# Reordering the opening of a fused attention and feed-forward kernel: token loads on two queues, fewer zero matmuls, shift products interleaved, scores of the first head moved forward, and the row of the condition vector moved to a later turn

## Chip, cores and metric

One core of a Trainium2 chip. The metric is the device time of one execution in microseconds (us); lower is better.

## The reference, cut to what matters

```python
mod = (_silu(c) @ w_mod).reshape(...)            # c: 1x1024, w_mod: 1024x6144
sa, ca, ga, sb, cb, gb = ...                     # shift, scale, gate of block A; the same of block B
h = _layernorm(x) * (1 + ca) + sa                # x: 2048 tokens x 1024
x = x + ga * attention(h)                        # 32 query heads, 4 key/value heads, last 512 keys
h = _layernorm(x) * (1 + cb) + sb
x = x + gb * swiglu_ffn(h)                       # 3584 wide
```

The opening has to compute the scale `ca` and shift `sa` from `c`, normalise the first 512 tokens, and start the query products of the first heads.

## The kernel before

`T.op(stream, emit, reads, writes)` records one instruction in its engine's stream, and the waits that its buffers demand. In these traces an instruction whose input is late holds up what stands behind it on its engine: in the kernel before TensorE's first instruction waits for the load of `c` until 3.69 us, and the nine zero matmuls behind it begin at 3.87 us. `mm` is one matmul (all at line 268 of the kernel before), `transpose` one TensorE transpose (line 272), `warm(n, b)` is n matmuls of zeros, recorded to keep TensorE busy. A wide matmul has 512 columns (128x512 in the views), a transpose 128, a product with a vector one. PSUM is the memory that matmuls write to, divided into banks (XB, QB and so on); an evacuation is the copy out of a bank, for which the next user of the bank waits here (1.47 us each in two places of the kernel before).

Two things below are called the row of `c`: the load of `c` itself (`c_row`, part 1 of the change), and the row that `row_task` makes of silu(c) for all partitions, with a copy on VectorE (part 5).

The loads, all from one queue:

```python
T.op(Q_x[0], lambda: SP.dma_start(x_res[:, 0, :], xf[0:P, :]), writes=[B_x[0]])
T.op(Q_c, lambda: SP.dma_start(c_row[:, :], c.rearrange("o (k p) -> (o k) p", p=P)), writes=[B_cT])
for t in range(1, TPC):
    T.op(Q_x[t], lambda: SP.dma_start(x_res[:, t, :], xf[t * P:(t + 1) * P, :]), writes=[B_x[t]])
# ... then scale weights (8 x 256 KB), query weights (2 x 512 KB), shift weights (4 x 512 KB), K, V ...
# TensorE's first instruction transposes c:
T.op(PE, lambda: TE.transpose(bank_bf(XB)[:, 0:DT], c_row[:, :], ident[0:DT, 0:DT]), ...)
```

The opening proper (statistics and normalisation on VectorE, GpSimd and ScalarE; transposes, scale products `mod_ca` and zero matmuls on TensorE; cut):

```python
warm(9, WB); stats(0, ...); aggr(0); stats(1, 1, 0); norm(0, 0, 0)
x_first(0)                     # 8 transposes of token tile 0
warm(6, WB) ... x_first(1); warm(2, WB)
for k in range(3):
    mod_ca(k); warm(2, WB)     # mod_ca(k): 8 one-column matmuls
... x_first(2) ... mod_ca(3), mod_ca(4) ... x_first(3) ... mod_ca(5..7)
warm(5, WB)
x_mod()                        # read the scale, evacuate the transposes into hT
```

Query products of heads 0 to 3 without the shift, then the shift products, then the shift is added to `hT` and its effect on the four queries (a bias `bq`, 32 one-column matmuls) to the queries:

```python
QB0 = [PVB, PVB + 1, SCB, QB]
for kc in range(DT):
    for h in range(LEAD + 1):
        mm(bank(QB0[h]), wq_s[0][:, kc, h * P:(h + 1) * P], hT[0][:, kc, :], ...)
for k in range(DT):
    mod_mm(wsa[:, k, :], B_wsa[k], k, MCOLS)           # shift products, 64 one-column matmuls
T.op(DVE, ... mod_bf[:, 0:DT] <- bank XB)              # "shift read", line 627
k_turn(0, SCB + 1)                                     # transposes of K
... 32 bias products; shift additions on VectorE (4), ScalarE (2), GpSimd (2); evacuations of the 4 queries
```

The turns of the attention loop. "Turn i" below is the value of `i`:

```python
rows = row_task(sc_row, B_scr, sc_bf[:, :], B_sc)      # silu(c) as a row on all partitions
bg.append(rows)
for i in range(1, NA + 2):
    ...
    if 2 <= i < 1 + Hkv:
        k_turn(i - 1, XB)                              # K transposes, PSUM bank XB
    if i == 5:
        add_ln1(1)                                     # normalisation of the next 512 tokens, in background
    if i + LEAD < NA:
        if (i + LEAD) % Hq == 0:
            finish(ln1[(i + LEAD) // Hq])
        qproj(i + LEAD, SCB + 3 if i == 1 else QB)     # 8 matmuls and an evacuation on VectorE
    ...
    if 0 <= i - 1 < NA:
        scores(i - 1)                                  # 4 matmuls, exponentials on ScalarE
    if 0 <= i - 2 < NA:
        pv(i - 2)                                      # 16 matmuls of 129 columns
    run_bg(1)                                          # one step of the first background task
```

`row_task` also puts its products into bank XB: four 128-column matmuls, then a copy on VectorE (line 584), twice.

The softmax here doesn't subtract the row's maximum and nothing guards it: scores larger than these inputs give would overflow.

Of the kernel before, what the change touches and what calls it, by code (L numbers as in the profile page):

```python
# [3 lines left out]
ALU = mybir.AluOpType  # L4
# [3 lines left out]
P = 128  # L8
# [122 lines left out]
def bass_adaLN_cond__sliding_block_cached__swiglu_ffn__prompt_kernel(  # L131
# [87 lines left out]
    def bank(b, n=512, off=0):  # L219
        return ps[:, b * 512 + off:b * 512 + off + n]  # L220
# [32 lines left out]
    QB = 4  # L253
# [4 lines left out]
    with nc.Block() as block:  # L258

        @block.gpsimd  # L260
        def _(g):
# [39 lines left out]
                    xf[ch * CH:(ch + 1) * CH, :].rearrange("(t p) d -> p t d", p=P)),  # L301
                     writes=B_x[ch * TPC:(ch + 1) * TPC])

            T.op(Q_x[0], lambda: SP.dma_start(x_res[:, 0, :], xf[0:P, :]), writes=[B_x[0]])  # L304
            T.op(Q_c, lambda: SP.dma_start(c_row[:, :], c.rearrange("o (k p) -> (o k) p", p=P)), writes=[B_cT])
            for t in range(1, TPC):
                T.op(Q_x[t], lambda: SP.dma_start(x_res[:, t, :], xf[t * P:(t + 1) * P, :]), writes=[B_x[t]])


            OFF_WO = 0  # L310
# [90 lines left out]
            def stats(t, sl, hf):  # L401
                T.op(DVE, lambda: V.bn_stats(st_[sl][:, hf * 6:hf * 6 + 6], x_res[:, t, hf * 512:hf * 512 + 512]),  # L402
                     reads=[B_x[t]], writes=[B_st[sl]])

            def aggr(sl):
                T.op(DVE, lambda: V.bn_aggr(mv[sl][:, :], st_[sl][:, :]), reads=[B_st[sl]], writes=[B_mv[sl]])  # L406
                T.op(POOL, lambda: g.tensor_scalar(rstd[sl], mv[sl][:, 1:2], eps, None, op0=ALU.add),  # L407
                     reads=[B_mv[sl]], writes=[B_rs[sl]])
                T.op(POOL, lambda: g.tensor_tensor(rstd[sl], rstd[sl], mhalf[:, 0:1], ALU.pow),  # L409
                     reads=[B_rs[sl], B_mh], writes=[B_rs[sl]])  # L410

            def norm(t, sl, ns):
                T.op(DVE, lambda: V.tensor_scalar(nsc4[ns], x_res[:, t, :], mv[sl][:, 0:1], rstd[sl],  # L413
                                                  op0=ALU.subtract, op1=ALU.mult),
                     reads=[B_x[t], B_mv[sl], B_rs[sl]], writes=[B_ns4[ns]])
# [41 lines left out]
            def warm(n, b):  # L457
                for _ in range(n):
                    mm(bank(b), zwarm[:, 0:P], zwarm, True, True, [B_zw], PB[b])
# [22 lines left out]
            def mod_ca(k):  # L482
                mod_mm(wca[k], B_wca[k], k, MCOLS)
# [3 lines left out]
            T.op(ACT, lambda: A.activation(nsc4[tl], x_res[:, tl, :], AF.Copy, accum_out=acc[:, 0:1]),  # L487
                 reads=[B_x[tl]], writes=[B_ns4[tl], B_acc])
            WB = PVB
            warm(9, WB)  # L490
            stats(0, 0, 0)
            stats(0, 0, 1)
            aggr(0)
            stats(1, 1, 0)
            norm(0, 0, 0)
            x_first(0)
            warm(6, WB)
            stats(1, 1, 1)
            aggr(1)
            T.op(POOL, lambda: g.tensor_scalar(nmean[:, :], acc[:, 0:1], -1.0 / D, None, op0=ALU.mult),  # L500
                 reads=[B_acc], writes=[B_nm])
            T.op(ACT, lambda: A.activation(nsc4[tl], x_res[:, tl, :], AF.Square, bias=nmean[:, 0:1], accum_out=acc[:, 1:2]),
                 reads=[B_x[tl], B_nm], writes=[B_ns4[tl], B_acc])
            stats(2, 2, 0)
            norm(1, 1, 1)
            x_first(1)
            warm(2, WB)
            for k in range(3):
                mod_ca(k)
                warm(2, WB)  # L510
            stats(2, 2, 1)
            T.op(DVE, lambda: V.bn_aggr(mv[2][:, :], st_[2][:, :]), reads=[B_st[2]], writes=[B_mv[2]])
            T.op(POOL, lambda: g.tensor_scalar(rstd[2], mv[2][:, 1:2], eps, None, op0=ALU.add),
                 reads=[B_mv[2]], writes=[B_rs[2]])
            T.op(POOL, lambda: g.tensor_scalar(rstd[tl], acc[:, 1:2], 1.0 / D, eps, op0=ALU.mult, op1=ALU.add),
                 reads=[B_acc], writes=[B_rs[tl]])
            T.op(POOL, lambda: g.tensor_tensor(rstd4[:, 2:4], rstd4[:, 2:4], mhalf[:, 0:2], ALU.pow),
                 reads=[B_mh], writes=[B_rs[2], B_rs[tl]])
            norm(2, 2, 2)
            x_first(2)  # L520
            warm(1, WB)
            T.op(DVE, lambda: V.tensor_scalar(nsc4[tl], x_res[:, tl, :], nmean[:, 0:1], rstd[tl],
                                              op0=ALU.add, op1=ALU.mult),
                 reads=[B_x[tl], B_nm, B_rs[tl]], writes=[B_ns4[tl]])
            for k in range(3, 5):
                mod_ca(k)
                warm(1, WB)
            x_first(3)
            for k in range(5, DT):
                warm(1, WB)  # L530
                mod_ca(k)
            warm(5, WB)
            x_mod()


# [59 lines left out]
            qT_s = [arena.at(OFF_QT + i * KB, [CH], BF16, [B_qT[i]]) for i in range(NQT)]  # L595
            Q_tr = [dq("q_tr%d" % i) for i in range(NOS)]

            def qproj(i, b=QB):
                ch, h = divmod(i, Hq)
                gidx = ch * HG + h // 4  # L600
                sl = gidx % NWQ
                hh = h % 4
                for kc in range(DT):
                    mm(bank(b), wq_s[sl][:, kc, hh * P:(hh + 1) * P], hT[ch % 2][:, kc, :], kc == 0, kc == DT - 1,
                       [B_wq[sl][kc // HK], B_hT[ch % 2][kc]], PB[b])
                qs = i % NQT
                T.op(DVE, lambda: V.tensor_copy(qT_s[qs], bank(b)), writes=[PB[b], B_qT[qs]])  # L607



            QB0 = [PVB, PVB + 1, SCB, QB]
            LEAD = 3
            for kc in range(DT):
                for h in range(LEAD + 1):
                    mm(bank(QB0[h]), wq_s[0][:, kc, h * P:(h + 1) * P], hT[0][:, kc, :], kc == 0, kc == DT - 1,
                       [B_wq[0][kc // HK], B_hT[0][kc]], PB[QB0[h]])
            for k in range(DT):
                mod_mm(wsa[:, k, :], B_wsa[k], k, MCOLS)

            def k_turn(gk, b):  # L620
                for kt in range(KT):
# [6 lines left out]
            k_turn(0, SCB + 1)  # L628
            kd, ks = k_evac(0, SCB + 1)
            T.op(ACT, lambda: A.activation(kd, ks, AF.Copy), writes=[PB[SCB + 1], B_kT[0]])  # L630
            for h in range(LEAD + 1):
                for kc in range(DT):
                    mm(bank(SCB + 2, 1, 2 * h), wq_s[0][:, kc, h * P:(h + 1) * P], mod_bf[:, kc:kc + 1],
                       h == 0 and kc == 0, kc == DT - 1, [B_wq[0][kc // HK], B_mode], PB[SCB + 2], skip=True)
            for dt in range(DT):
                d = hT[0][:, dt, :]
                if dt < 4:
                    T.op(DVE, lambda: V.tensor_scalar(d, d, mod_bf[:, dt:dt + 1], None, op0=ALU.add),  # L638
                         reads=[B_mode], writes=[B_hT[0][dt]])
                elif dt < 6:  # L640
                    T.op(ACT, lambda: A.activation(d, d, AF.Identity, bias=mod_bf[:, dt:dt + 1]),
                         reads=[B_mode], writes=[B_hT[0][dt]])
                else:
                    T.op(POOL, lambda: g.tensor_scalar(d, d, mod_bf[:, dt:dt + 1], None, op0=ALU.add),
                         reads=[B_mode], writes=[B_hT[0][dt]])
            T.op(DVE, lambda: V.tensor_copy(bq[:, :], psap((SCB + 2) * 512, [[2, LEAD + 1]])), writes=[PB[SCB + 2], B_bq])  # L646
            for h in (0, 2, 3, 1):
                if h < 2:
                    T.op(DVE, lambda: V.tensor_scalar(qT_s[h], bank(QB0[h]), bq[:, h:h + 1], None, op0=ALU.add),
                         reads=[B_bq], writes=[PB[QB0[h]], B_qT[h]])  # L650
                else:
                    T.op(ACT, lambda: A.activation(qT_s[h], bank(QB0[h]), AF.Identity, bias=bq[:, h:h + 1]),
                         reads=[B_bq], writes=[PB[QB0[h]], B_qT[h]])

            B_ex = [_Buf("ex%d" % i) for i in range(NEX)]
            ex_s = [arena.at(OFF_EX + i * 4 * KB, [KT, CH], BF16, [B_ex[i]]) for i in range(NEX)]
# [90 lines left out]
            LOADX = {19: 2, 40: 3}  # L747
            LOADT = {Hq + 2 + (9 * n) // 4: n for n in range(NL)}
            LOADO = {5 + (21 * p) // 8: p for p in range(8)}
            rows = row_task(sc_row, B_scr, sc_bf[:, :], B_sc)  # L750
            bg.append(rows)
            for i in range(1, NA + 2):
                ch, h = divmod(i, Hq)
                if i % 4 == 1:
# [7 lines left out]
                if 2 <= i < 1 + Hkv:  # L762
                    k_turn(i - 1, XB)
                    kd, ks = k_evac(i - 1, XB)
                    T.op(DVE, lambda: V.tensor_copy(kd, ks), writes=[PB[XB], B_kT[i - 1]])
                    if i == Hkv:
                        for b_ in B_hT[1]:
                            for kb in B_kn:
                                b_.absorb(kb)
                if i == 5:  # L770
                    add_ln1(1)
                if h == 2 and 1 <= ch < NCH - 1:
# [3 lines left out]
                if i + LEAD < NA:  # L776
                    if (i + LEAD) % Hq == 0:
                        finish(ln1[(i + LEAD) // Hq])
                    qproj(i + LEAD, SCB + 3 if i == 1 else QB)
                if 7 <= i < 7 + DT:  # L780
                    mod_mm(wga[:, i - 7, :], B_wga[i - 7], i - 7, GCOLS)
                    if i == 6 + DT:
# [18 lines left out]
                    oproj_mm(NCH - 1, 0, QB, 8 * n, 8 * n + 8)  # L801
                elif n >= 3:
                    oproj_mm(NCH - 1, 1, XB, 8 * (n - 3), 8 * (n - 3) + 8)
                if 0 <= i - 1 < NA:
                    scores(i - 1)
                if 0 <= i - 2 < NA:
                    pv(i - 2)
# [154 lines left out]
```

## Time and profile before

| | kernel before |
|---|---|
| median of 3 runs | 1283.01 us (1282.88 to 1283.18) |
| span of the profiled execution | 1282.1 us (that execution took 1283.94) |
| TensorE busy | 1264.0 us, 99% |
| first TensorE instruction | 3.69 us |
| first query product | 17.53 us |
| shift read | 27.03 us |
| K transposes of turn 4 | 44.13 us |

The page of the kernel before: its span, the busy time of each engine (us, share of the span, instructions), and from its fourth part the shares of the chain that ended last:

```profile
span 1282.1 us, 17720 instructions
...
PE 1264.0 (99%) x7513; PEld 646.4 (50%) x7655; DVE 477.4 (37%) x881; ACT 340.2 (27%) x384; POOL 44.5 (3%) x103
...
PE 98%; issue 1%; DVE 1%; DMA 0%; SPq 0%
```

TensorE is the bound, and it is on the chain nearly always. A change can only win where TensorE waits, does something useless or runs at a lower clock; that is the opening. The chain of waits of the kernel before, in order of time (start us, length us, what held the chain):

```profile
1.18 2.46 DMA c_row<-in_c_dram
...
3.87 3.95 PE ps L268 x9
...
17.53 0.59 PE ps L268 x2
...
37.12 0.69 DVE arena L689
37.81 0.61 DVE arena L584
...
38.55 0.38 PE ps L272 x4
...
48.06 6.94 PE ps L268 x55
```

The chain begins with the wait for the row of `c` (2.46 us); nine zero matmuls take 3.95 us, 0.44 us each, against 0.216 us later, so they ran at half the later speed (called cold below). At 37.1 and 42.5 us the chain leaves TensorE: it waits for two VectorE operations in a row, and the second (line 584) is the copy of the `c` row, after which the K transposes may reuse bank XB. The view of waits of the kernel before for 36 to 46 us (engine, waiting tile and line, what it waited for: us in total, times, longest us) adds this up:

```profile
PE ps L272 <- DVE arena L584: 2.9, 2, 1.5
```

The kernel before in one-microsecond windows (window, length, then for each engine busy us and instruction count, the granted TensorE clock as a share of full speed, DMA share, GB/s):

```profile
28.00:29.00 1.00, 0.86 (x11) 0.34 (x8) 1.00 (x3) 0.98 (x2) 1.00 (x1) 1.00 1.21 260
29.00:30.00 1.00, 0.76 (x3) 0.31 (x4) 0.96 (x4) 0.71 (x2) 1.00 (x2) 0.88 0.59 95
30.00:31.00 1.00, 0.98 (x3) 0.18 (x2) 0.69 (x2) 0.98 (x2) 0.91 (x3) 0.50 0.85 218
31.00:32.00 1.00, 1.00 (x4) 0.30 (x2) 0.68 (x1) 0.85 (x1) 1.00 (x2) 0.50 1.08 384
32.00:33.00 1.00, 1.00 (x6) 0.47 (x4) 0.01 (x1) 0.82 (x1) 1.00 (x3) 0.50 1.09 373
33.00:34.00 1.00, 1.00 (x8) 0.59 (x7) 0.42 (x1) 0.91 (x2) 0.22 (x1) 0.91 1.04 351
```

The clock fell to 0.50 near 29.8 us and was back at 33.2; this is called the half clock below. TensorE was recorded busy for 0.63, 0.74, 0.86 and 0.76 us of the four microseconds from 26 to 30. Half a clock for 3.4 us of 1282 us is 0.13%, so a run with it shows a mean clock of 0.999 and one without it 1.000.

### The profile page before, as it was taken

To read this page: it belongs to the slowest core of one execution; us is meant where nothing else is said; L and a number is where in the kernel's file an instruction comes from. 1 tells how busy PE (TensorE), PEld (TensorE's weight loads), DVE (VectorE), ACT (ScalarE), POOL (GpSimd) and SP (SyncE) were. 2 spreads that over 40 slices of the span, in tenths; PEclk is the share of its full clock that TensorE was granted. 3 is DMA by queue.
4 is the path that set the end of the run, shared out by engine and by line. 5 is a ranking of instruction groups with operands and counts; after the bars stand their busy time and mean duration, and the time that the engine had idled before them with its cause. 6 is when DMAs were issued, how large, how long until landed. Compare 5 with 4: busy or idle time off the path is not lost.

```text
span 1282.1 us, 17720 instructions
## 1 busy us (share of the span) xinstructions
PE 1264.0 (99%) x7513; PEld 646.4 (50%) x7655; DVE 477.4 (37%) x881; ACT 340.2 (27%) x384; POOL 44.5 (3%) x103
## 2 busy tenths in 40 slices
PE   8999999999999999999999999999999999999999
PEld 4565545555445554455554444444444444444444
DVE  4455314765137652265422331233222331221222
ACT  3555402555015551055520111011100111011100
POOL 2120000000000010000000000000000000000000
PEclk9999999999999999999999999999999999999999
DMA  9799402976108841055351974046421654035200
GB/s 316 202 230 272 108 1 40 217 139 148 34 17 162 174 105 46 1 122 118 71 152 60 288 243 131 17 136 176 132 74 34 200 152 131 17 109 170 66 9 25
DMA packets 234830, 155.31 MB, mean 121 GB/s; under 512 B 129024, under 2 KB 220032, under 8 KB 234752
## 3 DMA queue, kind: packets, MB, share of 16 engines
q1 hardware_dynamic: 176512, 95.45, 31.0%
q10 hardware_dynamic: 58240, 58.72, 14.5%
q8 instruction: 60, 0.98, 0.3%
q14 instruction: 18, 0.15, 0.0%
HBM read 119.54 MB, written 4.19 MB: 97 GB/s over the span
## 4 chain that ended last, share of the span: by engine, by line
PE 98%; issue 1%; DVE 1%; DMA 0%; SPq 0%
PE ps L268 98%; PE ps L272 0%; DMA c_row<-in_c_dram 0%; DVE arena L638 0%; DVE arena L689 0%; DVE arena L584 0%; DVE rl L686 0%; DVE tmp L708 0%; DVE arena L710 0%; SPq L304 0%; DVE arena L474 0%; PE ps L393 0%; DVE gain L454 0%; DVE mod_bf L468 0%; DVE gain_f L470 0%
## 5 line engine op out<-in xcount | busy, mean ns | idle before, releaser
L268 PE MATMUL ps<-arena 128*128 128x512 bf16 (+1 forms) x7240 | 1257.3, 333 | 8.0 <-DVE bq L646 0.2
L268 PEld LDWEIGHTS ps<-arena 128*128 128x128 bf16 x7382 | 636.3, 98 | 619.9 <-issue 3.6
L668 ACT ACTIVATE arena<-ps 128x1024 bf16<-128x1024 f32 x256 | 261.9, 1023 | 356.9 <-PE ps L268 345.1
L891 ACT ACTIVATE arena<-ps 128x512 bf16<-128x512 f32 x112 | 66.9, 597 | 506.2 <-PE ps L268 506.2
L892 DVE TENSOR_TENSOR arena<-ps,arena 128x512 bf16<-128x512 f32 x112 | 77.5, 692 | 276.2 <-PE ps L268 276.2
L708 DVE TENSOR_TENSOR tmp<-ps,rowb 128x512 f32<-128x512 f32 (+1 forms) x65 | 44.4, 683 | 319.1 <-PE ps L268 319.1
L607 DVE CAST arena<-ps 128x512 bf16<-128x512 f32 x124 | 85.7, 692 | 58.6 <-PE ps L268 58.6
L689 DVE TENSOR_TENSOR arena<-ps,rl 128x512 bf16<-128x512 f32 x128 | 88.5, 691 | 4.7 <-DVE rl L686 0.2
L686 DVE RECIPROCAL rl<-ps 128x4 f32<-128x4 f32 x128 | 23.3, 182 | 120.4 <-PE ps L268 120.4
L402 DVE BATCH_NORM_STATS2 st<-x_res 128x6 f32<-128x512 bf16 x62 | 42.3, 682 | 3.5 <-DMA x_res<-in_A_x_dram 3.5
L407 POOL TENSOR_SCALAR rstd<-mv 128x1 f32<-128x1 f32 x30 | 6.7, 222 | 911.1 <-DVE mv L406 911.1
L561 DVE SCALAR_TENSOR_TENSOR arena<-arena 128x1024 bf16<-128x1024 bf16 x24 | 29.2, 1215 | 0.0
L710 DVE TENSOR_TENSOR arena<-tmp,x_res 128x512 bf16<-128x512 f32 (+1 forms) x33 | 22.3, 676 | 1.1
L710 DVE TENSOR_TENSOR x_res<-tmp,x_res 128x512 bf16<-128x512 f32 x32 | 22.1, 692 | 1.1
L418 DVE TENSOR_SCALAR arena<-arena,gain,mod_bf 128x512 bf16<-128x512 bf16 x56 | 20.3, 405 | 0.0
L409 POOL TENSOR_TENSOR rstd<-rstd,mhalf 128x1 f32<-128x1 f32 x30 | 17.0, 568 | 2.5
L413 DVE TENSOR_SCALAR nsc<-x_res,mv,rstd 128x1024 bf16<-128x1024 bf16 x30 | 16.1, 538 | 1.0 <-POOL rstd L409 1.0
L576 POOL TENSOR_SCALAR arena<-arena,c 128x128 bf16<-128x128 bf16 x24 | 14.1, 606 | 7.0 <-PE ps L268 6.7
L268 PEld LDWEIGHTS ps<-sc_bf,arena 128*128 128x128 bf16 x192 | 7.1, 96 | 3.4
L268 PE MATMUL ps<-sc_bf,arena 128*128 128x1 bf16 x192 | 7.2, 163 | 0.1
L406 DVE BATCH_NORM_AGGREGATE mv<-st 128x2 f32<-128x12 f32 x30 | 6.3, 209 | 1.0
L272 PE MATMUL ps<-arena 128*128 128x128 bf16 x32 | 2.9, 228 | 2.9 <-DVE arena L584 2.9
(53 smaller groups left out, 42.2 us busy)
## 6 DMA issues: line engine op xcount, KB each, us to landing
arena<-in_A_wq_dram SPq DMA_DIRECT2D x31, 1024.0 KB, 5.7
arena<-in_B_w_gate_dram ACTq DMA_DIRECT2D x28, 1024.0 KB, 5.5
arena<-in_B_w_up_dram ACTq DMA_DIRECT2D x28, 1024.0 KB, 8.1
arena<-in_A_wo_dram SPq DMA_DIRECT2D x8, 1024.0 KB, 6.5
arena<-in_B_w_down_dram SPq DMA_DIRECT2D x7, 1024.0 KB, 8.3
out_dram<-arena SPq DMA_DIRECT2D x15, 256.0 KB, 2.0
x_res<-in_A_x_dram SPq DMA_DIRECT2D x3, 1024.0 KB, 7.5
arena<-in_w_mod_dram SPq DMA_DIRECT2D x8, 256.0 KB, 5.5
```

The lines of the kernel that those rows point to most:

```text
L268: T.op(PE, lambda: TE.matmul(out_ap, lhsT, rhs, start=start, stop=stop, skip_group_check=skip), reads=reads, writes=[bank_buf])
L402: T.op(DVE, lambda: V.bn_stats(st_[sl][:, hf * 6:hf * 6 + 6], x_res[:, t, hf * 512:hf * 512 + 512]), reads=[B_x[t]], writes=[B_st[sl]])
L418: T.op(DVE, lambda: V.tensor_scalar(dst[:, dt, :], dst[:, dt, :], gain[gi][:, dt:dt + 1], mod_bf[:, ccol + dt:ccol + dt + 1], op0=ALU.mult ...
L561: T.op(DVE, lambda: V.scalar_tensor_tensor(mt[n % 2], mt[n % 2], 1.0, sc_row, op0=ALU.mult, op1=ALU.mult, accum_out=mcol[:, n:n + 1]), rea ...
L607: T.op(DVE, lambda: V.tensor_copy(qT_s[qs], bank(b)), writes=[PB[b], B_qT[qs]])
L668: T.op(ACT, lambda: A.activation(ex_s[es][:, 2 * kp:2 * kp + 2, :], banks2(SCB + 2 * kp), AF.Exp, scale=att_scale), writes=[PB[SCB + 2 * k ...
L686: T.op(DVE, lambda: V.reciprocal(rl[r][:, :].rearrange("p (a b) -> p a b", a=2), psap(PVB * 512 + P, [[512, 2], [130, 2]])), writes=both + ...
L689: T.op(DVE, lambda: V.tensor_tensor(o_s[os_].rearrange("p (a b) d -> p a b d", a=2), psap(PVB * 512, [[512, 2], [130, 2], [1, P]]), rlb, A ...
L708: T.op(DVE, lambda: V.tensor_tensor(tmp[s][:, 0:n], bank(b, n), rowb[ri][:, c0:c0 + n], ALU.mult), reads=[B_row[ri]], writes=[PB[b], B_tmp ...
L710: T.op(DVE, lambda: V.tensor_tensor(dst[:, c0:c0 + n], tmp[s][:, 0:n], x_res[:, t, c0:c0 + n], ALU.add), reads=[B_tmp[s], B_x[t]], writes= ...
L891: T.op(ACT, lambda: A.activation(sg_s[ss], bank(gb), AF.Silu), writes=[PB[gb], B_sg[ss]])
L892: T.op(DVE, lambda: V.tensor_tensor(guT[:, ft, :], bank(ub), sg_s[ss], ALU.mult), reads=[B_sg[ss]], writes=[PB[ub], B_gu[ft]])
```

## The change

The intent: get TensorE to the attention loop earlier. Five parts:

1. Token tiles 1 and 3 are loaded from the scalar engine's queue, 0 and 2 from the sync engine's; the row of `c` goes third in the sync queue.
2. 24 zero matmuls instead of 34 in the opening; the statistics of each tile stand together on VectorE.
3. Shift products 0 to 3 go between the query products; five zero matmuls around the bias products; GpSimd has no shift additions any more.
4. In turn 1 the scores of head 0 stand ahead of the fifth query, which uses bank QB instead of a score bank.
5. The row of `c` is made in turn 17 instead of turns 1 to 3.

```diff
-            T.op(Q_x[0], lambda: SP.dma_start(x_res[:, 0, :], xf[0:P, :]), writes=[B_x[0]])
-            T.op(Q_c, lambda: SP.dma_start(c_row[:, :], c.rearrange("o (k p) -> (o k) p", p=P)), writes=[B_cT])
-            for t in range(1, TPC):
-                T.op(Q_x[t], lambda: SP.dma_start(x_res[:, t, :], xf[t * P:(t + 1) * P, :]), writes=[B_x[t]])
+            Q_xa = [dq("q_xa%d" % i, A) for i in range(2)]
+            for t in range(TPC):
+                q = Q_xa[t // 2] if t % 2 else Q_x[t]
+                T.op(q, lambda: (A if t % 2 else SP).dma_start(x_res[:, t, :], xf[t * P:(t + 1) * P, :]), writes=[B_x[t]])
+                if t == 2:
+                    T.op(Q_c, lambda: SP.dma_start(c_row[:, :], c.rearrange("o (k p) -> (o k) p", p=P)), writes=[B_cT])
...  (opening: 34 zero matmuls become 24, not counting the five below; statistics of a tile together; cut)
+            def mod_sa(k2):
+                for k in (2 * k2, 2 * k2 + 1):
+                    mod_mm(wsa[:, k, :], B_wsa[k], k, MCOLS)
+
             for kc in range(DT):
                 for h in range(LEAD + 1):
                     mm(bank(QB0[h]), wq_s[0][:, kc, h * P:(h + 1) * P], hT[0][:, kc, :], kc == 0, kc == DT - 1,
                        [B_wq[0][kc // HK], B_hT[0][kc]], PB[QB0[h]])
-            for k in range(DT):
-                mod_mm(wsa[:, k, :], B_wsa[k], k, MCOLS)
+                if kc == 3:
+                    mod_sa(0)
+                elif kc == 6:
+                    mod_sa(1)
+            mod_sa(2)
+            mod_sa(3)
...
+            warm(2, SCB + 3)
             for h in range(LEAD + 1):
                 ...  (32 bias products)
+            warm(3, SCB + 3)
...  (shift additions and evacuations: 7 on VectorE, 1 on ScalarE, none on GpSimd; order 4 shifts, bias, head 0, 3 shifts, head 1; cut)
-            rows = row_task(sc_row, B_scr, sc_bf[:, :], B_sc)
-            bg.append(rows)
...
+                if i == 17:
+                    bg.insert(0, row_task(sc_row, B_scr, sc_bf[:, :], B_sc))
...
-                    qproj(i + LEAD, SCB + 3 if i == 1 else QB)
+                    if i == 1:
+                        scores(0)
+                    qproj(i + LEAD)
...
-                if 0 <= i - 1 < NA:
+                if 1 <= i - 1 < NA:
                     scores(i - 1)
```

The recorded order of instructions shows that part 5 has one more effect. Background tasks take one step a turn; three more steps ahead of `ln1[1]` mean that its last two pairs of modulations stand together in turn 29, directly ahead of the query product that reads them. In the kernel before they ended two turns earlier.

More of the change, by code (lines that the diff above doesn't have):

```diff
@@ L489, in _, with stats_only, rstd_of @@
             WB = PVB
-            warm(9, WB)
-            stats(0, 0, 0)
-            stats(0, 0, 1)
-            aggr(0)
-            stats(1, 1, 0)
-            norm(0, 0, 0)
-            x_first(0)
-            warm(6, WB)
-            stats(1, 1, 1)
-            aggr(1)
+            def stats_only(t):
+                stats(t, t, 0)
+                stats(t, t, 1)
+                T.op(DVE, lambda: V.bn_aggr(mv[t][:, :], st_[t][:, :]), reads=[B_st[t]], writes=[B_mv[t]])
+            def rstd_of(t, src, rb, m):
+                T.op(POOL, lambda: g.tensor_scalar(rstd[t], src, m, eps, op0=ALU.mult, op1=ALU.add), reads=[rb], writes=[B_rs[t]])
+                T.op(POOL, lambda: g.tensor_tensor(rstd[t], rstd[t], mhalf[:, 0:1], ALU.pow), reads=[B_mh], writes=[B_rs[t]])
+            stats_only(0)
+            rstd_of(0, mv[0][:, 1:2], B_mv[0], 1.0)
+            stats_only(1)
+            rstd_of(1, mv[1][:, 1:2], B_mv[1], 1.0)
             T.op(POOL, lambda: g.tensor_scalar(nmean[:, :], acc[:, 0:1], -1.0 / D, None, op0=ALU.mult),
@@ L503, in _ @@
                  reads=[B_x[tl], B_nm], writes=[B_ns4[tl], B_acc])
-            stats(2, 2, 0)
+            norm(0, 0, 0)
+            stats_only(2)
+            rstd_of(2, mv[2][:, 1:2], B_mv[2], 1.0)
+            rstd_of(tl, acc[:, 1:2], B_acc, 1.0 / D)
             norm(1, 1, 1)
-            x_first(1)
-            warm(2, WB)
-            for k in range(3):
-                mod_ca(k)
-                warm(2, WB)
-            stats(2, 2, 1)
-            T.op(DVE, lambda: V.bn_aggr(mv[2][:, :], st_[2][:, :]), reads=[B_st[2]], writes=[B_mv[2]])
-            T.op(POOL, lambda: g.tensor_scalar(rstd[2], mv[2][:, 1:2], eps, None, op0=ALU.add),
-                 reads=[B_mv[2]], writes=[B_rs[2]])
-            T.op(POOL, lambda: g.tensor_scalar(rstd[tl], acc[:, 1:2], 1.0 / D, eps, op0=ALU.mult, op1=ALU.add),
-                 reads=[B_acc], writes=[B_rs[tl]])
-            T.op(POOL, lambda: g.tensor_tensor(rstd4[:, 2:4], rstd4[:, 2:4], mhalf[:, 0:2], ALU.pow),
-                 reads=[B_mh], writes=[B_rs[2], B_rs[tl]])
             norm(2, 2, 2)
-            x_first(2)
-            warm(1, WB)
             T.op(DVE, lambda: V.tensor_scalar(nsc4[tl], x_res[:, tl, :], nmean[:, 0:1], rstd[tl],
@@ L524, in _ @@
                  reads=[B_x[tl], B_nm, B_rs[tl]], writes=[B_ns4[tl]])
+            warm(9, WB)
+            x_first(0)
+            warm(4, WB)
+            x_first(1)
+            for k in range(3):
+                mod_ca(k)
+                warm(1, WB)
+            x_first(2)
             for k in range(3, 5):
@@ L528, in _ @@
             x_first(3)
-            for k in range(5, DT):
-                warm(1, WB)
-                mod_ca(k)
-            warm(5, WB)
+            warm(1, WB)
+            mod_ca(5)
+            warm(1, WB)
+            mod_ca(6)
+            mod_ca(7)
+            warm(4, WB)
             x_mod()
@@ L596, in _, with qproj @@
             Q_tr = [dq("q_tr%d" % i) for i in range(NOS)]
-            def qproj(i, b=QB):
+            def qproj(i):
                 ch, h = divmod(i, Hq)
@@ L603, in qproj @@
                 for kc in range(DT):
-                    mm(bank(b), wq_s[sl][:, kc, hh * P:(hh + 1) * P], hT[ch % 2][:, kc, :], kc == 0, kc == DT - 1,
-                       [B_wq[sl][kc // HK], B_hT[ch % 2][kc]], PB[b])
+                    mm(bank(QB), wq_s[sl][:, kc, hh * P:(hh + 1) * P], hT[ch % 2][:, kc, :], kc == 0, kc == DT - 1,
+                       [B_wq[sl][kc // HK], B_hT[ch % 2][kc]], PB[QB])
                 qs = i % NQT
-                T.op(DVE, lambda: V.tensor_copy(qT_s[qs], bank(b)), writes=[PB[b], B_qT[qs]])
+                T.op(DVE, lambda: V.tensor_copy(qT_s[qs], bank(QB)), writes=[PB[QB], B_qT[qs]])
             QB0 = [PVB, PVB + 1, SCB, QB]
             LEAD = 3
+            def mod_sa(k2):
+                for k in (2 * k2, 2 * k2 + 1):
+                    mod_mm(wsa[:, k, :], B_wsa[k], k, MCOLS)
             for kc in range(DT):
@@ L634, in _, with shift @@
                        h == 0 and kc == 0, kc == DT - 1, [B_wq[0][kc // HK], B_mode], PB[SCB + 2], skip=True)
-            for dt in range(DT):
+            warm(3, SCB + 3)
+            def shift(dt, on_act=False):
                 d = hT[0][:, dt, :]
-                if dt < 4:
-                    T.op(DVE, lambda: V.tensor_scalar(d, d, mod_bf[:, dt:dt + 1], None, op0=ALU.add),
-                         reads=[B_mode], writes=[B_hT[0][dt]])
-                elif dt < 6:
+                if on_act:
                     T.op(ACT, lambda: A.activation(d, d, AF.Identity, bias=mod_bf[:, dt:dt + 1]),
@@ L643, in _, with q_out @@
                 else:
-                    T.op(POOL, lambda: g.tensor_scalar(d, d, mod_bf[:, dt:dt + 1], None, op0=ALU.add),
+                    T.op(DVE, lambda: V.tensor_scalar(d, d, mod_bf[:, dt:dt + 1], None, op0=ALU.add),
                          reads=[B_mode], writes=[B_hT[0][dt]])
-            T.op(DVE, lambda: V.tensor_copy(bq[:, :], psap((SCB + 2) * 512, [[2, LEAD + 1]])), writes=[PB[SCB + 2], B_bq])
-            for h in (0, 2, 3, 1):
-                if h < 2:
+            def q_out(h, on_act=False):
+                if on_act:
+                    T.op(ACT, lambda: A.activation(qT_s[h], bank(QB0[h]), AF.Identity, bias=bq[:, h:h + 1]),
+                         reads=[B_bq], writes=[PB[QB0[h]], B_qT[h]])
+                else:
                     T.op(DVE, lambda: V.tensor_scalar(qT_s[h], bank(QB0[h]), bq[:, h:h + 1], None, op0=ALU.add),
                          reads=[B_bq], writes=[PB[QB0[h]], B_qT[h]])
-                else:
-                    T.op(ACT, lambda: A.activation(qT_s[h], bank(QB0[h]), AF.Identity, bias=bq[:, h:h + 1]),
-                         reads=[B_bq], writes=[PB[QB0[h]], B_qT[h]])
+            for dt in range(4):
+                shift(dt)
+            shift(4, True)
+            T.op(DVE, lambda: V.tensor_copy(bq[:, :], psap((SCB + 2) * 512, [[2, LEAD + 1]])), writes=[PB[SCB + 2], B_bq])
+            q_out(0)
+            q_out(2, True)
+            q_out(3, True)
+            for dt in range(5, DT):
+                shift(dt)
+            q_out(1)
             B_ex = [_Buf("ex%d" % i) for i in range(NEX)]
```

## The prediction

> **What bounds it now.** The page's chain that ended last is 98% TensorE. From the sixth attention turn (48.06 us in the chain) TensorE repeats without gaps, so the change can win only before that. The 48 us hold: a start waiting for the c row (chain: 3.69 us); 34 zero 512-column matmuls; 0.6 us idle from the last scale product (16.4) to the first query product (17.53); a stretch of one-column products, 24.6 to 28.3 us; two waits of 1.47 us for the row copy on VectorE (waits view), which shares a PSUM bank with the K transposes; and a granted clock of 0.50 for about 3.4 us, 29.8 to 33.2 (one-microsecond windows), after the stretch with few wide matmuls. Nine wide matmuls there took 3.75 us, not 1.95.
>
> **The change, costed.**
> 1. Ten zero matmuls fewer net, nine of them ahead of the scale read; at 0.216 us warm about 1.8 us.
> 2. Against it: the c row, TensorE's first wait, now queues behind two token tiles while the scalar queue carries two more. [...] Before, 1 MB of tokens moved at about 280 GB/s from 2 us and the last tile landed at 6.6, so I estimate c at 5.5 to 6.3 instead of 3.64: TensorE starts 2 us later. Much is hidden: before, matmuls ran cold (0.43 us) to about 9.3 us anyway. [...] Net gain of 1 and 2 at the scale read: 0.8 us (range -0.9 to 1.8). VectorE's reordered statistics are not limiting.
> 3. Shift products moved between query products: they spread wide matmuls into the thin stretch. With five zero matmuls they should mostly avoid the half-clock window (about 1.6 us).
> 4. Scores of head 0 before the fifth query: wide work restarts 3 us after the shift read (four shift adds 1.95, copy 0.14, evacuation 0.70) instead of 1.3, but exponentials start 2 us earlier and every score bank is free in time. New wait: the sixth query, on the same bank as the fifth, about 0.75 us for the evacuation.
> 5. The c row moved to turn 17: the two 1.47 us waits go. Its products (0.4 us) just move.
> 6. New cost in that move: background steps run one a turn; three more ahead of the second chunk's normalisation leave its last two modulation pairs together in turn 29. Four at 0.36 us stand just ahead of the query needing them: an estimated 0.75 us stall, once.
>
> From the shift read to turn 5 I add up 17.4 us against 21.0: 3.6 us gained. With 0.8, less 0.44 (row products), 0.75, and 0.4 for a possible half-clock window: about 3 us.
>
> **Prediction: 1280.1 us, eight in ten between 1278.3 and 1282.0; faster by over 2% 0.005, within 2% 0.99, slower by over 2% 0.005.**
>
> **What would show it.** Right: TensorE's first matmul near 6 us; first query product about 16.7; shift read near 26; no wait on the row copy in turns 2 to 4; sixth turn starting near 43.5; one wait on modulation near turn 29; no gaps otherwise.
> **Wrong if:** the c row lands early (gain near 4.5 us)[...]; the half clock returns at the first scores; or query weights come late.

The sum is 0.8 + 3.6 - 0.44 - 0.75 - 0.4 = 2.8 us, put as about 3 us; 1280.1 us is 2.9 us below the 1283.01 us of the kernel before.

## The result, and the profile after

The changed kernel: 1281.10 us median of 4 runs (1280.66 to 1282.11), the kernel before beside it 1282.95 us (1282.70 to 1283.18): 1.9 us less. The ratio is 0.9987 with a 95% interval of 0.9969 to 1.0004. A ratio is the mean time of one kernel's fast runs over that of the other's of the same rounds, so it is not quite the ratio of the medians quoted. A second series (after_again below) gave 0.9985 (0.9972 to 0.9998).

The page of the changed kernel:

```profile
span 1278.9 us, 17849 instructions
...
PE 1267.8 (99%) x7650; PEld 644.5 (50%) x7650; DVE 477.3 (37%) x884; ACT 339.5 (27%) x383; POOL 41.8 (3%) x102
...
PE 99%; DVE 0%; DMA 0%; issue 0%; SPq 0%
```

The chain of waits of the changed kernel:

```profile
1.64 4.35 DMA c_row<-in_c_dram
...
6.22 3.60 PE ps L268 x9
...
16.88 0.59 PE ps L268 x2
...
27.78 0.76 DVE arena L664
...
28.68 2.76 PE ps L268 x12
...
31.47 0.70 DVE arena L611
...
32.22 3.67 PE ps L268 x28
...
39.83 10.21 PE ps L268 x79
```

The load of `c` now takes 4.35 us from issue to landing, against 2.46. The nine zero matmuls still take 3.60 us. No copy of the row stands in the chain of turns 2 to 4. But two VectorE pieces are new at 27.78 and 31.47 us, each followed by a TensorE start. The view of waits of the changed kernel for 26 to 46 us says what they are:

```profile
PE ps L268 <- DVE arena L664: 0.7, 1, 0.7
...
PE ps L268 <- DVE arena L611: 0.6, 1, 0.6
```

Line 664 is the evacuation of head 0's query, for which the scores of head 0 wait; line 611 is the evacuation of the fifth query, for whose bank the sixth waits. In the one-microsecond windows of the changed kernel the clock stays up, although TensorE is busy for only 0.32 us between 28 and 29:

```profile
28.00:29.00 1.00, 0.32 (x2) 0.22 (x3) 1.00 (x4) 1.00 (x2) 0.00 (x0) 1.00 0.69 136
29.00:30.00 1.00, 1.00 (x7) 0.41 (x5) 0.98 (x3) 0.98 (x2) 0.00 (x0) 1.00 0.69 188
30.00:31.00 1.00, 1.00 (x6) 0.46 (x5) 0.00 (x0) 0.99 (x2) 0.00 (x0) 1.00 1.08 382
31.00:32.00 1.00, 0.66 (x6) 0.31 (x4) 0.53 (x1) 0.91 (x2) 0.00 (x0) 1.00 1.10 380
```

Later comes the new stall. The timeline of VectorE in the kernel before (start us, busy us, engine, line, operation, out<-in, shapes, count) has the modulations of the second chunk two at a time; the last two pairs:

```profile
124.35 0.72 DVE L418 TENSOR_SCALAR arena<-arena,gain,mod_bf 128x512 bf16<-128x512 bf16 x2
...
127.84 0.73 DVE L418 TENSOR_SCALAR arena<-arena,gain,mod_bf 128x512 bf16<-128x512 bf16 x2
```

The timeline of VectorE in the changed kernel has four in a row:

```profile
130.60 1.38 DVE L420 TENSOR_SCALAR arena<-arena,gain,mod_bf 128x512 bf16<-128x512 bf16 x4
```

The timeline of the weight loads (PEld) in the changed kernel, which stand just ahead of their matmuls, shows that they wait for these modulations one by one (in brackets the idle time before, and what ended it):

```profile
131.07 0.10 PEld L268 LDWEIGHTS ps<-arena 128*128 128x128 bf16 x1 [0.96 <-DVE arena L420]
131.39 0.10 PEld L268 LDWEIGHTS ps<-arena 128*128 128x128 bf16 x1 [0.23 <-DVE arena L420]
131.71 0.10 PEld L268 LDWEIGHTS ps<-arena 128*128 128x128 bf16 x1 [0.23 <-DVE arena L420]
132.03 2.04 PEld L268 LDWEIGHTS ps<-arena 128*128 128x128 bf16 x22 [0.23 <-DVE arena L420]
```

It helps to cut every trace at two points that all kernels share, the shift read and the start of the K transposes of turn 4 (from the timeline views). "To the end" is the span less the second point.

| profiled kernel | shift read | from it to turn 4 | turn 4 to the end |
|---|---|---|---|
| before | 27.03 | 17.10 | 1237.97 |
| before_again | 26.27 | 16.67 | 1237.96 |
| after | 26.09 | 13.36 | 1239.45 |
| after_again | 26.33 | 13.36 | 1239.41 |

So the changed kernel gains 3.3 to 3.7 us in the middle stretch, gives 1.45 to 1.5 us back later, and what it gains up to the shift read depends on which profile one takes: 0.70 to 0.94 us against the first, -0.06 to 0.18 us against the second.

### The profile page after: what moved, and what is told of

Read it like the earlier page. It is cut to its first block, busy times and chain, and to the rows that moved or that the text cites. A ratio compares the mean times of both kernels' runs of the same rounds, so it can differ in the third digit from the quotient of the medians.

```text
span 1278.9 us, 17849 instructions
## 1 busy us (share of the span) xinstructions
PE 1267.8 (99%) x7650; PEld 644.5 (50%) x7650; DVE 477.3 (37%) x884; ACT 339.5 (27%) x383; POOL 41.8 (3%) x102
## 4 chain that ended last, share of the span: by engine, by line
PE 99%; DVE 0%; DMA 0%; issue 0%; SPq 0%
PE ps L268 99%; DMA c_row<-in_c_dram 0%; PE ps L272 0%; SPq L307 0%; DVE arena L664 0%; DVE arena L611 0%; DVE arena L712 0%; DVE tmp L731 0%; DVE arena L733 0%; DVE arena L476 0%; DVE arena L420 0%; DVE rl L709 0%; DVE gain L456 0%; PE ps L395 0%; DVE mod_bf L470 0%
```

## Experiments

Twelve kernels, all correct, each in five rounds (six runs for the last) beside the kernel before. The kernels of one call ran on one chip: the first four, the next four, and the next three together with the last beside a largely shared set of runs of the kernel before.

| kernel | median us | range | kernel before | ratio (95%) | mean clock of the runs |
|---|---|---|---|---|---|
| before_again | 1282.94 | 1282.75 to 1283.24 | 1283.14 | 0.9999 (0.9986 to 1.0011) | 0.998 to 1.0 |
| row_only | 1280.70 | 1280.60 to 1280.80 | 1283.14 | 0.9982 (0.9969 to 0.9994) | 0.999 to 1.0 |
| c_first | 1280.17 | 1279.76 to 1280.82 | 1283.14 | 0.9978 (0.9966 to 0.9991) | 1.0 |
| two_steps | 1280.42 | 1279.68 to 1281.19 | 1283.14 | 0.9980 (0.9966 to 0.9994) | 1.0 |
| after_again | 1281.24 | 1280.42 to 1282.03 | 1283.17 | 0.9985 (0.9972 to 0.9998) | 1.0 |
| old_scores | 1279.84 | 1279.40 to 1280.29 | 1283.17 | 0.9974 (0.9961 to 0.9986) | 1.0 |
| q5_bank | 1280.35 | 1280.25 to 1281.26 | 1283.17 | 0.9980 (0.9967 to 0.9992) | 1.0 |
| no_zeros | 1284.16 | 1283.96 to 1284.57 | 1283.17 | 1.0008 (0.9994 to 1.0022) | 0.997 |
| row_back | 1282.90 | 1282.60 to 1283.72 | 1282.91 | 1.0000 (0.9987 to 1.0014) | 1.0 |
| before_zeros | 1283.43 | 1282.36 to 1283.64 | 1282.91 | 1.0001 (0.9989 to 1.0014) | 0.999 to 1.0 |
| best_mix | 1277.92 | 1277.40 to 1278.53 | 1282.91 | 0.9960 (0.9948 to 0.9973) | 1.0 |
| shift_back | 1282.73 | 1282.11 to 1283.32 | 1282.95 | 0.9997 (0.9985 to 1.0010) | 0.999 |

The intervals of the ratios are wide for effects of 1 us (0.0008). Where two variants are compared below, their medians and ranges are given, and the stretches of their traces, which repeat far better than the totals:

| profiled kernel | shift read | from it to turn 4 | turn 4 to the end |
|---|---|---|---|
| row_only | 26.99 | 12.49 | 1239.42 |
| c_first | 25.33 | 13.36 | 1239.41 |
| two_steps | 26.17 | 13.35 | 1238.48 |
| old_scores | 26.41 | 12.21 | 1239.38 |
| q5_bank | 26.33 | 12.79 | 1239.38 |
| no_zeros | 27.06 | 15.88 | 1239.46 |
| row_back | 26.83 | 17.06 | 1238.01 |
| before_zeros | 26.42 | 17.42 | 1237.96 |
| best_mix | 26.05 | 12.21 | 1238.44 |
| shift_back | 27.68 | 14.42 | 1239.40 |

### before_again: the kernel before, unchanged

> The kernel before, unchanged, as a control and for a second profile. Theory H (the half-clock window of about 3.4 us near 30 us belongs to this kernel's opening, because the stretch before it holds few wide matmuls): the profile shows a granted clock of 0.5 again between 25 and 37 us, and the nine wide matmuls near 29 us take 3 us or more. Rival ([...]): no half clock this time, and the span is 0.8 to 1.5 us below 1282.1. Ratio to the kernel before 1.000 within 0.0005 either way.

Level with itself. The half clock came again (0.50 from 27.8 to 31.2 us), so it belongs to this kernel. But this profile's shift read is 0.76 us earlier than the first one's, and its span 1.2 us shorter, as the rival had it: the first profile was a slow execution. Of the 33 timed and profiled executions of the kernel before, 9 had a mean clock of 1.000 and a mean time of 1283.09 us, 21 had 0.999 and 1283.12 us, 3 had 0.998 and 1282.72 us. In this kernel the runs with a half clock are not slower.

### row_only: part 5 alone

```diff
-rows = row_task(sc_row, B_scr, sc_bf[:, :], B_sc)
-bg.append(rows)
 for i in range(1, NA + 2):
+    if i == 17:
+        bg.insert(0, row_task(sc_row, B_scr, sc_bf[:, :], B_sc))
```

> The kernel before with only the row of c moved to turn 17. If the row's two waits were worth what the waits view says: two waits of 1.47 us and 0.44 us of products leave the first turns, 0.44 us and one stall of about 1 us in turn 29 (four modulations ahead of the query) come later, net 1.9 us faster, ratio 0.9985. Rival (the waits were only slack and something else refills them): under 0.5 us, ratio above 0.9996.

It is 2.4 us faster than the kernel before, more than the whole change, which is 1.9 us faster. The K transposes in row_only's timeline of TensorE follow each other every 3.72 us, against 5.77 and 5.58 us in the kernel before (32.78, 38.55, 44.13):

```profile
32.04 0.39 PE L272 MATMUL ps<-arena 128*128 128x128 bf16 x4
...
35.76 0.39 PE L272 MATMUL ps<-arena 128*128 128x128 bf16 x4
...
39.48 0.39 PE L272 MATMUL ps<-arena 128*128 128x128 bf16 x4
```

So the two waits of 1.47 us were worth about 1.86 us each, products included, and nothing refilled them.

### c_first: the row of `c` first in the queue

```diff
+T.op(Q_c, ... c_row ...)
 for t in range(TPC):
     ...
-    if t == 2:
-        T.op(Q_c, ... c_row ...)
```

> The changed kernel with the row of c issued first, ahead of the token tiles. TensorE's first matmul near 3.6 us instead of 6.04. If the late start costs little, because matmuls are cold until about 9.5 us and the second normalised tile is there only at 10.0 us: first query product 0.5 to 0.9 us earlier than the 16.88 us of the changed kernel and the whole 0.5 to 0.9 us faster than it. Rival 1 (all 2.4 us of the late start are lost): 2 us faster or more. Rival 2 (nothing is lost): under 0.2 us.

TensorE starts at 2.84 us instead of 6.04. From c_first's timeline of TensorE, its first instruction and the transposes of the first two token tiles:

```profile
2.84 0.18 PE L394 MATMUL ps<-arena,c_row 8*128 8x8 bf16 x1 [2.84 <-DMA c_row<-in_c_dram]
...
8.21 0.62 PE L272 MATMUL ps<-arena,nsc 128*128 128x128 bf16 x8 [1.32 <-DVE nsc L414]
...
10.20 0.62 PE L272 MATMUL ps<-arena,nsc 128*128 128x128 bf16 x8 [0.50 <-DVE nsc L414]
```

The start 3.2 us earlier moves the shift read by 0.76 us against the first profile of the changed kernel and by 1.00 us against the second; the median is 1.1 us lower than after_again's, and the ranges overlap (up to 1280.82, from 1280.42). Where the rest of the 3.2 us goes is in the same view: the first transposes now wait 1.32 us for the first normalised tile, and the second set 0.50 us. The first of the three expectations is the nearest; in these traces the late start costs about a quarter to a third of itself.

### two_steps: two more background steps

```diff
-run_bg(1)
+run_bg(2 if i in (20, 21) else 1)
```

> The changed kernel with one more background step in turns 20 and 21, so that the second chunk's modulations end two turns before the query that reads them. If the stall in turn 29 (query products waiting for four modulations, 0.96 us in the chain) is a new cost of the moved row: 0.9 to 1.0 us faster than the changed kernel, no wait on a modulation near 131 us. Rival (the stall only moves, or the extra VectorE work in turns 20 and 21 holds an evacuation up): under 0.3 us.

From turn 4 to the end the trace takes 1238.48 us, against 1239.45: 0.97 us less, and the chain of waits of two_steps from 100 to 170 us is one piece of TensorE work:

```profile
99.86 70.32 PE ps L268 x491
```

The median is 0.8 us below after_again's. The stall of turn 29 is a cost of the moved row, and it is avoidable.

### after_again: the changed kernel, unchanged

> The changed kernel, unchanged, as a control on the same chip as the next three. Median 1280.6 to 1281.6 us, ratio to the kernel before 0.9985 (0.9980 to 0.9990), wider spread than the kernel before (about 1.5 us), mean granted clock 1.0 in all runs: no half-clock window.

As expected. The spread of 1.6 us is much wider than row_only's 0.2 us.

### old_scores: turn 1 in the old order

```diff
-if i == 1:
-    scores(0)
-qproj(i + LEAD)
+qproj(i + LEAD, SCB + 3 if i == 1 else QB)
 ...
-if 1 <= i - 1 < NA:
+if 0 <= i - 1 < NA:
     scores(i - 1)
```

> The changed kernel with the old order in turn 1: fifth query first, on the fourth score bank, then the scores of head 0. Theory S (the new order lost about 0.9 us: TensorE idles 0.75 us for the evacuation of head 0 and 0.56 to 0.77 us for the bank of the fifth query): K transposes of turn 3 near 34.7 us instead of 35.73, the whole 0.8 to 1.1 us faster than the changed kernel. Rival (the new order is a gain, because the exponentials start earlier, as the change intends): slower by 0.5 us or more. Second rival (no matter): within 0.2 us.

1.4 us faster than after_again on the same chip, ranges not overlapping. The chain of waits of old_scores from 28 us on:

```profile
28.10 0.75 DVE arena L664
28.85 0.79 DVE arena L656 x3
29.64 0.66 DVE arena L664
30.30 0.61 DVE arena L611
...
30.95 0.39 PE ps L268
31.34 0.22 PE ps L272 x4
```

While VectorE evacuates head 0 (28.10) and adds the last shifts (28.85), TensorE works on the fifth query, of whose eight products the first five need no late shift; only one score matmul then waits, 0.22 us. In the changed order TensorE idles 0.75 us for head 0 first and 0.56 us for the bank after. Part 4 is a loss, 1.15 us in the traces (13.36 to 12.21).

### q5_bank: another bank for the sixth query

```diff
-qproj(i + LEAD)
+qproj(i + LEAD, PVB if i == 2 else QB)
```

> The changed kernel with the sixth query product accumulated in the first value bank, which is free, instead of the bank that the fifth query has just left. Theory S: the wait of 0.56 to 0.77 us for the evacuation of the fifth query goes, K transposes of turn 3 near 35.0 us instead of 35.73, 0.6 to 0.8 us faster than the changed kernel. Rival (the score banks or the value bank make the next wait of the same length): under 0.2 us.

0.9 us faster by the medians, 0.57 us in the middle stretch: the second of the two waits, as named. The rest of the median's difference lies within the scatter.

### no_zeros: the five zero matmuls taken out

```diff
-warm(2, SCB + 3)
 ... 32 bias products ...
-warm(3, SCB + 3)
```

> The changed kernel without the five zero matmuls around the query bias products. Theory H (zero matmuls keep the half clock away, which is worth about 1.6 us as the prediction had it): mean clock 0.999 in some runs and those runs 0.5 us or more slower than the others. Rival, suggested by the kernel before, whose runs at clock 0.999 and at 1.000 have the same mean time of 1283.1 us: the half clock may return, but runs with it are within 0.2 us of runs without it, and as the two zeros ahead of the bias products are gone the kernel is 0 to 0.3 us faster than the changed one.

Both theories missed the size: 2.9 us slower than after_again by the medians, with a mean clock of 0.997 in all five runs. The one-microsecond windows of no_zeros:

```profile
28.00:29.00 1.00, 0.23 (x10) 0.14 (x6) 0.81 (x4) 0.65 (x2) 0.00 (x0) 0.65 0.77 155
29.00:30.00 1.00, 0.35 (x1) 0.14 (x2) 1.00 (x4) 1.00 (x2) 0.00 (x0) 0.50 0.39 65
...
34.00:35.00 1.00, 1.00 (x6) 0.45 (x5) 0.03 (x1) 0.00 (x0) 0.00 (x0) 0.50 1.03 387
35.00:36.00 1.00, 0.59 (x6) 0.26 (x4) 0.99 (x2) 0.00 (x0) 0.00 (x0) 0.93 0.91 338
```

The clock is at half from 28.30 us to 35.13, nearly seven microseconds, twice as long as in the kernel before. TensorE is busy only 0.23 and 0.35 us of the two microseconds from 28 to 30, most of which lie after the fall, so this idle time did not begin the half clock. The 12 wide matmuls behind them (5.28 us instead of 2.75) have no wait left to hide in: the middle stretch is longer by the same 2.5 us (15.88 against 13.36). The rest of this trace's loss lies ahead of the shift read. Five matmuls of zeros, 1.1 us of TensorE time put into idle time, save 2.5 us in the traces and 2.9 us by the medians.

### row_back: the change without part 5

```diff
+rows = row_task(sc_row, B_scr, sc_bf[:, :], B_sc)
+bg.append(rows)
 for i in range(1, NA + 2):
-    if i == 17:
-        bg.insert(0, row_task(...))
```

> The changed kernel with the row of c put back into turns 1 to 3, all else of the change kept. Theory R (the move of the row is the whole net gain; the rest of the change gains about 0.9 us up to the shift read and loses it again to the new order of scores and the late start): 2.2 to 2.5 us slower than the changed kernel, so 1283.4 to 1283.8 us, level with the kernel before or up to 0.6 us slower. The prediction on record instead puts the opening at 0.8 us and the half clock at 1.2 us net: then this kernel would be 1 us or more faster than the kernel before.

1282.90 us beside 1282.91 us: parts 1 to 4 together are worth nothing, within a scatter of 1.1 us. The waits for the copy of the row are back (38.32 and 43.89 us, 1.47 us each), as the timeline of TensorE in row_back shows for the first:

```profile
38.32 0.38 PE L272 MATMUL ps<-arena 128*128 128x128 bf16 x4 [1.47 <-DVE arena L588]
```

The middle stretch is 3.70 us longer, the last one 1.44 us shorter.

### before_zeros: the five zero matmuls in the kernel before

```diff
+warm(2, SCB + 3)
 ... 32 bias products ...
+warm(3, SCB + 3)
```

> The kernel before with only the five zero matmuls of the change around the query bias products. Mean clock 1.000 in all runs (in the kernel before it is 0.999 in most). If the half clock cost the kernel before 1.6 us as the prediction had it: 1.2 to 1.6 us faster where the kernel before ran at 0.999. If it fell mostly into waits for the shift additions (the row_only trace, same program up to there, has no half clock and still waits 0.25 and 0.40 us): 0 to 0.4 us faster, within noise.

A miss on the clock: three of five runs still had 0.999, and the trace shows the half clock from about 27.5 to 31. Those three took 1283.4 to 1283.6 us, the two at 1.000 took 1282.4 and 1282.6. In time it is level with the kernel before. The zeros alone do not hold the clock.

### best_mix: the three losses undone together

The edits of c_first, two_steps and old_scores, in one kernel.

> The changed kernel with the three losses undone together: row of c first in the queue, the fifth query ahead of the scores of head 0, two more background steps in turns 20 and 21. If the three are independent, 0.8 + 1.4 + 0.9 us: 1278.1 us, 1277.7 to 1278.6, 5 us faster than the kernel before, ratio 0.996. If they overlap: above 1279 us.

1277.92 us: 3.3 us faster than after_again, the sum of 1.1, 0.8 and 1.4 us, and 5.0 us faster than the kernel before, more than two and a half times the gain of the change. So the three losses add up, within the scatter. Its trace has the shift read at 26.05 us only, because the clock rose late in that execution (four zero matmuls near 9 us took 1.91 us, against 1.03 in the changed kernel).

### shift_back: the shift products after all query products

```diff
-                if kc == 3:
-                    mod_sa(0)
-                elif kc == 6:
-                    mod_sa(1)
+            mod_sa(0)
+            mod_sa(1)
             mod_sa(2)
```

> The changed kernel with all 64 shift products after the query products, as before, and everything else of the change kept, the five zero matmuls too. If the interleaving keeps the half clock away together with the zeros (the kernel before with the zeros alone still had it in 3 of 5 runs): mean clock below 1.000 in 2 or more of 5 runs, and those runs 1 us or more slower than the changed kernel's 1281.2. If the zeros alone do it in this order: clock 1.000 in all runs and the time within 0.3 us of the changed kernel.

All six runs at 0.999, and 1.5 us slower than after_again. The half clock is back with the zeros in place, as the one-microsecond windows of shift_back show:

```profile
30.00:31.00 1.00, 0.73 (x2) 0.28 (x3) 1.00 (x5) 0.98 (x3) 0.00 (x0) 0.50 0.62 121
```

So the two halves of part 3, the interleaving and the zeros, are both needed here: without either one the clock falls (mean clock 0.997 in no_zeros, 0.999 here, 1.000 with both).

## Why the prediction was right or wrong

**The total.** 1280.1 us predicted, 1281.10 measured, inside the range of 1278.3 to 1282.0. The gain was 1.9 us, not 2.9.

**The step that was mis-sized** is the term of the opening, "Net gain of 1 and 2 at the scale read: 0.8 us (range -0.9 to 1.8)". The scale read is the VectorE copy that waits for the last scale product. Four traces of the old opening have it at 15.65 to 16.42 us, mean 16.07; eight of the changed one (c_first and best_mix left out) at 15.77 to 17.07, mean 16.26. So on average 0.2 us was lost there, within the scatter, and not 0.8 us gained. From the scale read to the shift read every trace takes 10.61 us (to 0.01 us) with the shift products behind the query products (shift_back too) and 10.32 us with them interleaved, so the interleaving gains 0.3 us, and at the shift read the two openings are level (means 26.68 and 26.61 us).

What failed in that term is "Much is hidden: before, matmuls ran cold (0.43 us) to about 9.3 us anyway", which holds the rise of the clock fixed. By the clock records of the traces (the first record, at full clock; ahead of it none stands, and wide matmuls took about 0.43 us) the clock rose at 7.07, 7.30, 9.26 and 9.29 us with the old opening and at 9.33 to 11.98 us in the seven traces of the changed one that have a record: in all eleven 3.3 to 5.9 us after TensorE's first instruction, which now comes 2.4 us later. The later the rise, the later the scale read (changed opening: 9.33 and 15.77, 9.83 and 16.01, 11.24 and 16.74, 11.98 and 17.07). With the rise near 9.3 us in both, the changed opening is 0.6 us ahead (15.77 against 16.38 and 16.42), not far from the forecast; in most traces of the changed opening the rise came later than that, and the gain is gone. That the later start is what makes the rise later is the author's reading: with the early start back, the first transposes took 0.62 us in c_first (at 8.21) but 1.03 in best_mix (at 7.99). The first profiles before and after had nearly the same rise (9.29 and 9.33), the latest of the one opening and the earliest of the other, so together they flatter the forecast; that was luck. The first profile before was also of a slow execution: it took 1283.94 us where the timed runs had a median of 1283.01, and that difference stood in the data. The direction of the two parts was right: the late row costs about what the fewer zeros gain (c_first: 0.76 to 1.00 us in the traces).

**The half clock** was put at "about 1.6 us" with 0.4 us taken off for its possible return. It never returned: all runs of the changed kernel are at 1.000. And in the kernel before it was worth less: row_only's middle stretch plus the 3.70 us of the row gives 16.19 us without half clock, against 16.67, 17.10 and 17.42 in the three profiles with it (the last is before_zeros), so 0.5 to 1.2 us, because part of the slowed matmuls would have waited for shift additions anyway (row_only, without a half clock, still waits 0.25 and 0.40 us there). In the timed runs of the kernel before no difference is seen; those of before_zeros differ by 1.0 us. What the prediction did not see is that the changed order makes the clock more valuable: there its loss costs 1.1 us (shift_back) to 2.5 us (no_zeros) in the middle stretch.

**The middle stretch**, 3.6 us gained "from the shift read to turn 5", came out at 3.3 to 3.7. Inside it, the row was worth 3.70 us (row_back against after) and the new order of scores lost 1.15 us (old_scores). The prediction had the mechanism of that loss, the later restart and the new wait for the sixth query's bank (0.75 us predicted, 0.56 in the waits view), but folded it into a sum and did not say that part 4 is a loss.

**The cost in turn 29**, predicted 0.75 us, is 0.97 us (two_steps), and with the products of the row 1.45 us are given back after turn 4, against 1.19 predicted.

**Events**, predicted and seen in the first profile after: first TensorE matmul near 6 (6.04), first query product 16.7 (16.88), shift read near 26 (26.09), no wait on the row copy in turns 2 to 4 (none), sixth turn near 43.5 (43.2), one wait near turn 29 (at 131 us). The hits on the first query product and the shift read are in part luck: in the seven other traces of the changed opening they came at 16.96 to 18.18 us and at 26.17 to 27.68 us.

**In one line:** the row's move is the change (2.4 us alone); the rest, zeros, interleaving, queues and order, cancels to 0.0 us (row_back) or, on top of the move, costs 0.5 us (after_again against row_only), because an interleaving and five zeros that hold the clock only pay for a late load of `c` and a worse order of scores. By the prediction's own terms the move was worth 2.2 us (two waits of 1.47 us less the stall of 0.75) and the rest about 0.6 us, against 2.4 and 0.0 measured. The two errors partly cancel in the total, so part of its nearness is luck too.

What stays open: how far the scatter of 1.6 us in the totals of the changed kernel is that of the clock's rise. The traces point there: from the shift read on, after and after_again agree within 0.05 us in each stretch, and all of the difference lies ahead of it, where the first set of transposes takes 0.61 us in some traces of the changed opening and 1.06 us in others. The timed runs have no traces, so it was not tested for them. It also stays open why runs of the kernel before with a half clock are no slower than those without. In two of the three traces of the old opening with one (before_again, before_zeros) the clock had also risen 2 us earlier than in row_only, which had none, and the shift read came 0.6 to 0.7 us earlier; that this is the whole reason is not shown.

## What to carry to other kernels

A change of many parts has to be taken apart even when its total is near the forecast: here one part made all the gain, one was a loss of over a microsecond, and undoing three of the losses more than doubled the gain. Look for waits in which two unrelated tasks share a PSUM bank, and when a background task is moved, count the steps that then stand ahead of the next deadline. Take an opening's time from several profiles, because the moment at which the TensorE clock rises moves it by a microsecond (rise at 9.33 to 11.98 us, scale read at 15.77 to 17.07), and zero matmuls were worth nothing in one order (before_zeros) and 2.5 to 2.9 us in another (no_zeros): count whether they hold the clock before relying on them.

## What else the traces show of the clock and the loads

- In these traces the recorded busy time does not tell where the clock falls. From 26 to 29 us TensorE was busy for 2.23 us in the kernel before (longest gap 0.62 us) and for 2.81 us in shift_back, and the clock fell at 29.8 and 29.0 us; in the changed kernel it was busy for 2.25 us and in row_only for 2.33 us, and the clock held. What decides it was not shown.
- In no_zeros the half clock lasted 6.83 us (28.30 to 35.13), against 3.4 us in the kernel before, although twelve wide matmuls ran one behind the other from 29.65 us on. Why it lasted twice as long was not shown.
- With token tiles on two queues 320 to 327 GB/s moved between 2 and 6 us (after, after_again, two_steps, q5_bank, c_first), and with one queue 263 to 304 (before, before_again, row_only, before_zeros). It was not isolated from the order of the transfers.
- The 2 KB of `c` took 4.35 us from issue to landing with two 256 KB tiles ahead of it in its queue and two more on the other, against 2.46 us behind one tile.
